# One row-tiled stretch a step for both score blocks, with the down products ahead of it, in a fused attention and GEGLU kernel

## The chip, the core and the metric

The kernel runs on one NeuronCore of a Trainium2 chip. The metric is the device time of one execution in microseconds. Five engines work side by side, each through its own instructions in order: TensorE (PE, with its weight loads shown as PEld), VectorE (DVE), ScalarE (ACT), GpSimd (POOL) and SyncE (SP), which here issues the DMAs. Matrix products land in PSUM, which has eight banks of 512 float32 words per partition. DVE and ACT empty them.

## What is computed

```python
g = sigmoid((x * gate_w).sum(-1, keepdims=True))     # x: 2048 x 576
a = A(x, wq, wk, wv, wo, beta)                       # 32 heads of 18, 4 segments of 512
b = (gelu(x @ w_gate) * (x @ w_up)) @ w_down         # inner width 4608
return g * a + (1 - g) * b

# A, for each segment s
logits = q @ k.T * scale + causal_mask               # 512 x 512 per head
a_dot  = softmax(logits) @ v
a_mem  = (phi(q) @ M) / (phi(q) @ z + 1e-6)          # memory of the segments before
o      = sigmoid(beta) * a_mem + (1 - sigmoid(beta)) * a_dot
M, z   = M + phi(k).T @ v, z + phi(k).sum()
# a = o @ wo
```

Inputs are float32. The kernel splits each float32 operand into a high and a low float16 word and adds three products (high by high, high by low, low by high).

## The kernel before

A first part projects q, k and v and makes the segment memories. Then comes the main part that the change touches: 72 calls of `step(v)`, two for each of the 36 strips of 128 columns of the inner width (`f, p = divmod(v, 2)`). Step v works on strip f and on token chunks c = 2p and e = 2p + 1, of 512 tokens each. Two strips, so four steps, are a block of weights: `fb, i4 = divmod(v, 4)`, with i4 = 0 to 3 the step's place in the block.

The gate and up products use sums and differences of weights and tokens (a Strassen-like scheme), collected in three PSUM banks: X (tag G), Y (tag U) and V. Each `product` call is six matmuls of 512 columns: two blocks of rows k by three word pairs. The last 64 rows of the width 576 come through `rest` (whole array, `x[:, 8]`) and `low_rests`: the low word of the weights takes only 64 of the array's 128 rows, so that two such products, on rows 0 to 63 and 64 to 127, can run beside each other. `gelu` (ACT) and `hidden` (DVE) finish the strip for chunks c and e in tiles g0 and g1 (`gl`, three buffers), and `hidden_pair` splits the result into words hh: the high one on ACT, the low one on POOL.

Into the steps is woven:

- **Down products** of the block before: `down`, six matmuls of 288 columns each into a `dn` bank (two buffers) and one DVE operation that adds the result to `acc`. Eight a step, through `chains`.
- **Attention.** In step v the head and half-sequence with k = v - LAG (LAG is 2) is worked on, with two score blocks a = 2k and b = 2k + 1. `scores` makes four products of 54 rows (three stacked words of 18) with 512, 384, 256 and 128 columns, on rows from 0 or from 64, so two run beside each other. `piece` on DVE adds the mask, takes the row maximum into `mx` and writes to `pf` (two buffers). `powers` is, on ACT, a small operation `mb` on the maxima and four exponentials in place in `pf`. `pair_rows` splits them into words `ph` (ACT the high, POOL the low one), `turn_rows` transposes these by two DMAs into `pt` (two buffers), `values` multiplies them with v into bank `pv` (20 matmuls of 37 columns for a block), and `normalize` (DVE) divides and adds to `ob`. `result_high` and `result_low` split finished rows of `ob`.
- **Weights** for the next strips: `weights_first` (POOL scales them in steps i4 = 0 and 2 and forms the sums in steps 1 and 3, with one scaling of `rawd` in each of steps 2 and 3), `weights_high` (ACT) and `weights_low` (POOL). `act_squares` (ACT) and `scales` (PE, DVE), in step 1 with `scales_out` (POOL), make their scales.

The order on PE, ACT, DVE and POOL is the order of the code (`manual_schedule`), by hand. DMAs on SP are placed by the scheduler. In a step before, low last rows of V and Y (L1095) and the scores of block a stand in one row-tiled stretch in mid-step, and low last rows of X and of Y's last term UG, with the scores of block b, in another at the end. The pieces of a are emptied in the same step, those of b at the start of the next, where the two `hidden` of the step before stand too (`end_pair`).

Of the kernel before, what the change touches and what calls it, by code (L numbers as in the profile page):

```python
# [13 lines left out]
OP = mybir.AluOpType  # L14
# [4 lines left out]
P = 128  # L19
D = 576  # L20
F = 4608
H = 32
DH = 18
L = 512
# [18 lines left out]
def kernel(ctx: ExitStack, tc: tile.TileContext, xs, wqk, wv, wo, wgu, wd, beta, out):  # L43
# [8 lines left out]
    def bank(tag, bufs=1, dt=F32):  # L52
        return ps.tile([P, 512 if dt == F32 else 1024], dt, name=tag, tag=tag, bufs=bufs)
# [77 lines left out]
    x16 = {}  # L131
# [758 lines left out]
    with tc.tile_pool(name="keep", bufs=2, side="right", reuse_waits="tile") as kp, ExitStack() as tail:  # L890
# [25 lines left out]
        def load_v(gg):  # L916
            if gg >= H // 2:
                return
            hf, g = divmod(gg, H // 4)
            vts[gg] = ap_.tile([P, 8, 4 * VC], F16, name="vt", bufs=2)  # L920
            sp.dma_start(vts[gg], vps[hf][:, g * 4 * VC : (g + 1) * 4 * VC].rearrange("(t p) c -> p t c", p=P))
# [11 lines left out]

        COL = [0, P, 3 * P, 6 * P, 10 * P]

        PIECES = ((3, 0), (2, 64), (1, 64), (0, 0))

        def scores(a):

            k, e = divmod(a, 2)  # L940
            q, kt = qts[k], kts[k]
            mx[a] = ap_.tile([P, 4], F32, name="mx", bufs=2)
            prob[a] = ap_.tile([P, 10 * P], F32, name="pf", bufs=2)
            put = []
            for i, (qi, r) in enumerate(PIECES):
                h, n = slice(r, r + 3 * DH), (qi + 1) * P
                o = bank("st" if i < 2 else "dn", 2)[:, :n]
                pe.matmul(o, q[h, e * L + qi * P : e * L + (qi + 1) * P], kt[h, e * L : e * L + n],  # L948
                          start=True, stop=True)
                put.append((qi, o))  # L950

            def piece(i):
                qi, ov = put[i]
                dve.tensor_tensor_reduce(prob[a][:, COL[qi] : COL[qi + 1]], ov, mask[:, L - (qi + 1) * P :],  # L954
                                         1.0, -3e38, OP.add, OP.max, mx[a][:, qi : qi + 1])

            return piece

        def powers(a):

            p = prob[a]
            b = ap_.tile([P, 4], F32, name="mb", bufs=2)
            c = 2 * (a // (2 * H)) + a % 2
            act.activation(b, mx.pop(a), AF.Copy, bias=LN256, scale=esc[:, 1, c : c + 1])  # L964
            for qi in (3, 0, 2, 1):
                r = p[:, COL[qi] : COL[qi + 1]]
                act.activation(r, r, AF.Exp, bias=b[:, qi : qi + 1], scale=esc[:, 0, c : c + 1])  # L967
# [12 lines left out]
        def turn_rows(a):  # L980
            prob.pop(a)
            t, h = turned_p[a], pairs16.pop(a)
            for i in range(2):
                sp.dma_start(t[:, 10 * i : 10 * i + 10], h[:, i], transpose=True)

        def values(a):
            kk, e = divmod(a, 2)
            if e == 0:
                pvb[kk] = bank("pv")
            o = pvb[kk]  # L990
            pr = turned_p.pop(a)
            v = vts[kk // 4]
            c0 = (kk % 4) * VC
            for qi in range(4):
                ov = o[:, (4 * e + qi) * VC : (4 * e + qi + 1) * VC]
                for kb in range(qi + 1):
                    for i in range(2):
                        pe.matmul(ov, pr[:, 10 * i + COL[qi] // P + kb], v[:, 4 * e + kb, c0 : c0 + VC],  # L998
                                  start=kb == 0 and i == 0, stop=kb == qi and i == 1)
# [54 lines left out]
        def chains(b, js):  # L1054
            for j in js:
                down(b, j // 2, j % 2)
                if j % 8 == 7:
                    for ff in (2 * b, 2 * b + 1):
                        hp.pop((ff, j // 8))
                        if j == 31:  # L1060
                            pair_d.pop(ff)
# [14 lines left out]
        def gl_tile():  # L1076
            return mp2.tile([P, L], F32, name="gl", bufs=3)

        def product(o, f, a, x, h, l, start=False, part=range(6)):

            w = pair_g[f]
            for n in part:
                k, (i, b) = n // 3, ((0, h), (0, l), (1, h))[n % 3]
                pe.matmul(o, w[:, i, (a + k) * P : (a + k + 1) * P], x[:, b + k],  # L1084
                          start=start and n == 0, stop=n == 5, skip_group_check=True)
# [11 lines left out]
        def weights_first(fb, i4):  # L1097
            n0 = 2 * fb
            if i4 == 0 and fb:
                scale_g(n0 + 1)  # L1100
            if i4 == 1 and fb:
                sums_g(n0 + 1)
            if i4 == 2 and fb:
                scale_g(n0 + 2)
                scale_d(n0)
            if i4 == 3 and fb:
                sums_g(n0 + 2)
                scale_d(n0 + 1)

        def weights_high(fb, i4):  # L1110
            n0 = 2 * fb
            high_g(n0 + 1 + i4 // 2, i4 % 2)
            if i4 >= 2:
                high_d(n0 + i4 - 2)
# [7 lines left out]
        def weights_load(fb, i4):  # L1122
            n0 = 2 * fb
            if i4 == 1:
                load_g(n0 + 4)
            if i4 == 2:
                load_d(n0 + 2)
            if i4 == 3:
                load_v(fb + 1)
                load_g(n0 + 5)  # L1130
                if not fb:
                    load_d(n0 + 3)
            if i4 == 0 and fb > 1:
                load_d(n0 + 1)

        def act_squares(v):

            fb, i4 = divmod(v, 4)
            todo = {0: ((fb + 1, 2 * fb, 2),),
                    1: ((fb + 1, 2 * fb + 3, 0), (fb + 1, 2 * fb + 3, 1), (fb + 1, 2 * fb + 1, 2)),  # L1140
                    2: ((fb + 2, 2 * fb + 4, 0), (fb + 2, 2 * fb + 4, 1))}
            todo = todo.get(i4, ()) if fb else ()
            if v == 4:
                todo += (2, 4, 0), (2, 4, 1)
            for b, f, i in todo:
                squares(b, f, i, act_square)
# [3 lines left out]
        def first_product(v):  # L1150
            f, p = divmod(v, 2)
            V = bank("V")
            product(V, f, S3, xt[p], 8, 10, True)
            return V
# [3 lines left out]
        def end_pair(between=()):  # L1158

            for i, g in enumerate(ends):  # L1160
                hidden(*g)
                if i == 0:
                    for put in between:
                        put()
            for f, c, o, g in ends:
                hidden_pair(f, c, g)
            ends.clear()

        def step(v):

            f, p = divmod(v, 2)
# [8 lines left out]

            done = (k - 5) // 4 if i4 == 3 and 0 <= (k - 5) // 4 < H // 2 else None
            low = (k - 6) // 4 if i4 == 0 and 0 <= (k - 6) // 4 < H // 2 - 1 else None
            first, middle = {3: ((), ()), 4: ((0,), (1,)), 5: ((2, 3), (4,))}.get(
                v, ((2 * k - 3,) * on(k - 2), (2 * k - 2,) * on(k - 1)))
            x1, x2_, t = x16[c], x16[e], xt[p]
            X, Y = bank("G"), bank("U")
            if v in ahead:
                V, g1 = ahead.pop(v), gl_tile()
                dve.tensor_copy(g1, V)
                end_pair()  # L1190
                act_squares(v)
            else:
                end_pair([lambda i=i: put(2 * k - 1, i) for i in (2, 3)])
                act_squares(v)
                V, g1 = first_product(v), gl_tile()
                dve.tensor_copy(g1, V)
# [12 lines left out]
            for w in {3: (B21, BR), 4: (T3, T4)}.get(v - LAST, ()):  # L1209
                low_w(w)  # L1210
            put(2 * k - 1, 1)
            if v < 4:
                put(2 * k - 1, 2)
                put(2 * k - 1, 3)
            puts.pop(2 * k - 1, None)
# [272 lines left out]
        LAG = 2  # L1488
        LAST = 2 * H + LAG + 1
        with tc.manual_schedule(engines=ORDERED):  # L1490
            for v in range(2 * NF):
                step(v)

                if v == LAST:
                    atn.close()
                    op_ = tail.enter_context(tc.tile_pool(name="outp", bufs=2, side="right", reuse_waits="tile"))
                if v >= LAST:
                    for t in {0: (0, 1), 1: (2, 3), 2: (4, 5), 3: (6,)}.get(v - LAST, ()):
                        turned(t)
                    if v < LAST + 2:  # L1500
                        finish(v - LAST)
            sums_high(1)
            sums_low(1)
            end_pair()


            fb = NB - 1
            for u in range(8):
                unit(u)
                for t in (2 * u + 7, 2 * u + 8):  # L1510
                    if t < 16:
                        turned(t)
                if u < 6:
                    sums_o(u + 2)
                    sums_high(u + 2)
                    sums_low(u + 2)
# [40 lines left out]
```

## Time and profile before

| | |
|---|---|
| Median of 3 runs | 1570.52 us (1570.18 to 1570.59) |
| The profiled execution | 1570.53 us, span 1568.8 us |
| TensorE clock granted | 1.00 |
| Matmuls | 11902 |
| Step start to step start, v = 8 to 65 | 18.22 to 18.36 us |
| A block of four steps | 73.03 us |
| DMA queue of SP, share of 16 engines | 72.3% |

Step starts are read as the first matmul of the product S3 into V in each step. A matmul's busy time in the profile includes its way through the array, so two that follow each other overlap; how often one starts is read from the chain of waits, which shows a run of matmuls with the time until the next one.

### The profile page before, as it was taken

How to read it: one execution, taken by the hardware profiler on the slowest of the kernel's cores; microseconds unless marked ns; L12 is line 12 of the kernel's file. 1: busy time of each engine (PE TensorE's matmuls, PEld its weight loads, DVE VectorE, ACT ScalarE, POOL GpSimd, SP SyncE). 2: the span in 40 equal slices, each digit the busy share in tenths (PEclk: the TensorE clock that was granted, in tenths of full speed). 3: DMA queues.
4: the chain of work that ended last, by engine and by line, in shares of the span. 5: the costliest groups of instructions: out<-in, count | busy, mean ns of one | idle time of the engine just before them, and what ended most of it. 6: DMA issues, size and time to landing. Idle time of an engine off the chain costs nothing.

```text
span 1568.8 us, 32695 instructions
## 1 busy us (share of the span) xinstructions
PE 1563.5 (100%) x11902; PEld 922.2 (59%) x11902; DVE 1142.5 (73%) x2995; ACT 1177.6 (75%) x1973; POOL 1219.1 (78%) x1164
## 2 busy tenths in 40 slices
PE   9999999999999999999999999999999999999999
PEld 6665754555555555555555555555555555555577
DVE  7688876777777777777777767777776777776766
ACT  6667648888879798888888887879888888874310
POOL 3344867888888879797978888887879797887774
PEclk9999999999999999999999999999999999999999
DMA  6633445787979797878788897969797889736162
GB/s 224 221 125 110 140 149 93 126 143 121 147 121 142 118 157 129 142 131 128 130 132 143 126 146 124 147 122 159 112 155 134 136 133 129 139 76 143 32 146 97
DMA packets 472305, 209.00 MB, mean 133 GB/s; under 512 B 427600, under 2 KB 437072, under 8 KB 471632
## 3 DMA queue, kind: packets, MB, share of 16 engines
q1 hardware_dynamic: 472144, 206.92, 72.3%
q8 instruction: 93, 1.52, 0.4%
q14 instruction: 68, 0.56, 0.1%
HBM read 90.99 MB, written 27.26 MB: 75 GB/s over the span
## 4 chain that ended last, share of the span: by engine, by line
PE 98%; ACT 1%; DMA 0%; DVE 0%; issue 0%; SPq 0%; ACTq 0%
PE dn L1044 27%; PE U L1084 18%; PE G L1084 12%; PE V L1084 12%; PE pv L998 4%; PE st L333 3%; PE U L1090 2%; PE G L333 2%; PE dn L342 2%; PE G L1095 1%; PE V L1095 1%; PE U L333 1%; PE st L948 1%; PE U L1437 1%; PE V L1090 1%; PE G L1090 1%
## 5 line engine op out<-in xcount | busy, mean ns | idle before, releaser
L1044 PE MATMUL dn<-paird,hh 128*128 128x288 f16 x3408 | 485.9, 286 | 0.0
L978 POOL TENSOR_TENSOR ph<-pf,ph 128x512 f16<-128x512 f32 (+1 forms) x256 | 353.9, 1404 | 166.6 <-ACT ph L977 166.5
L1084 PEld LDWEIGHTS <-pairg 128*128 128x128 f16 x3024 | 274.8, 98 | 282.3 <-issue 33.0
L1044 PEld LDWEIGHTS <-hh 128*128 128x128 f16 x3456 | 337.7, 98 | 155.8 <-issue 0.2
L1052 DVE SCALAR_TENSOR_TENSOR acc<-dn,ev,acc 128x288 f32<-128x288 f32 x536 | 275.1, 514 | 65.9 <-PE dn L1044 65.4
L967 ACT ACTIVATE pf<-pf,mb,esc 128x512 f32<-128x512 f32 (+3 forms) x512 | 292.9, 642 | 7.0 <-ACT mb L964 0.4
L1084 PE MATMUL G<-x,pairg 128*128 128x512 f16 x864 | 222.0, 380 | 0.5 <-DVE gl L1066 0.4
L1084 PE MATMUL U<-xt,pairg 128*128 128x512 f16 x864 | 210.0, 379 | 0.0
L313 POOL TENSOR_TENSOR pairg<-raw,pairg 128x640 f16<-128x640 f32 (+2 forms) x144 | 175.1, 1238 | 4.0 <-ACT pairg L309 4.0
L1071 POOL TENSOR_TENSOR hh<-gl,hh 128x512 f16<-128x512 f32 x144 | 163.9, 1158 | 16.2 <-ACT hh L1070 16.2
L977 ACT ACTIVATE ph<-pf 128x512 f16<-128x512 f32 (+1 forms) x256 | 172.4, 720 | 0.0
L309 ACT ACTIVATE pairg<-raw 128x640 f16<-128x640 f32 (+2 forms) x144 | 89.9, 651 | 103.3 <-POOL raw L303 54.7
L1250 DVE COPY gl<-U 128x512 f32<-128x512 f32 x72 | 49.8, 692 | 160.8 <-PE U L1084 148.2
L954 DVE CUSTOM_DVE_ANT_0 pf<-st,mask 128x512 f32<-128x512 f32 (+1 forms) x256 | 156.9, 614 | 0.0
L278 POOL TENSOR_SCALAR raw<-raw,sc 128x640 f32<-128x640 f32 x72 | 135.5, 1894 | 0.0
L1084 PE MATMUL U<-x,pairg 128*128 128x512 f16 x432 | 126.9, 378 | 0.0
L1074 ACT ACTIVATE gl<-gl,sc 128x512 f32<-128x512 f32 x144 | 96.6, 715 | 39.4 <-DVE gl L1283 28.2
L954 DVE CUSTOM_DVE_ANT_0 pf<-dn,mask 128x256 f32<-128x256 f32 (+1 forms) x256 | 80.7, 353 | 59.9 <-PE dn L948 59.9
L1070 ACT ACTIVATE hh<-gl 128x512 f16<-128x512 f32 x144 | 85.7, 619 | 28.1 <-DVE gl L1066 27.9
L1084 PE MATMUL V<-xt,pairg 128*128 128x512 f16 x432 | 105.7, 381 | 0.0
L1084 PE MATMUL V<-x,pairg 128*128 128x512 f16 x432 | 104.8, 378 | 0.0
L998 PEld LDWEIGHTS <-pt 128*128 128x128 f16 x2560 | 83.2, 96 | 6.3
(304 smaller groups left out, 2627.4 us busy)
## 6 DMA issues: line engine op xcount, KB each, us to landing
raw<-in_wgu_dram SPq DMA_DIRECT2D x36, 640.0 KB
rawd<-in_wd_dram SPq DMA_DIRECT2D x36, 288.0 KB
qk<-stage SPq DMA_DIRECT2D x36, 256.0 KB
qt<-qk SPq DMA_DIRECT2D x128, 72.0 KB
kt<-qk SPq DMA_DIRECT2D x128, 72.0 KB
vp<-vstage SPq DMA_DIRECT2D x16, 296.0 KB
vt<-vp SPq DMA_DIRECT2D x16, 296.0 KB
qt<-qk SPq DMA_DIRECT2D x128, 36.0 KB
```

Of the source, the lines that this page charges most:

```text
L278: pool.tensor_scalar(r, r, scl[f // 2][0][:, 0:1], None, OP.mult)
L313: pool.tensor_tensor(spot(f, *p, 1), raw_g[f][:, p[0] : p[1]], spot(f, *p, 0), OP.subtract)
L954: dve.tensor_tensor_reduce(prob[a][:, COL[qi] : COL[qi + 1]], ov, mask[:, L - (qi + 1) * P :], 1.0, -3e38, OP.add, OP.max, mx[a][:, qi : q ...
L967: act.activation(r, r, AF.Exp, bias=b[:, qi : qi + 1], scale=esc[:, 0, c : c + 1])
L977: act.activation(h[:, 0, cols], p[:, cols], AF.Copy)
L978: pool.tensor_tensor(h[:, 1, cols], p[:, cols], h[:, 0, cols], OP.subtract)
L998: pe.matmul(ov, pr[:, 10 * i + COL[qi] // P + kb], v[:, 4 * e + kb, c0 : c0 + VC], start=kb == 0 and i == 0, stop=kb == qi and i == 1)
L1044: pe.matmul(o[:, :NH], hh[:, a, q * P : (q + 1) * P], w[:, b, n * NH : (n + 1) * NH], start=i == 0, stop=i == 5)
L1052: dve.scalar_tensor_tensor(av, o[:, :NH], ev, av, OP.mult, OP.add)
L1071: pool.tensor_tensor(hh[:, 1], t, hh[:, 0], OP.subtract)
L1074: act.activation(t, o, AF.Gelu_apprx_tanh, scale=scl[f // 2][0][:, 2 + c : 3 + c])
L1084: pe.matmul(o, w[:, i, (a + k) * P : (a + k + 1) * P], x[:, b + k], start=start and n == 0, stop=n == 5, skip_group_check=True)
```

## The change

A new function `paired_step(v)` takes the place of `step(v)` for v from LAG + 3 = 5 to LAST - 2 = 65 (LAST is 67). In it:

- Low last rows of V and Y, all products of both score blocks, and the low last rows of X stand in one row-tiled stretch. Pieces share banks: the narrow ones lie two to a bank, over both `st` banks, both `dn` banks and `pv`.
- Low last rows of UG are made by `rest` on the whole array.
- All eight down products and the value products of blocks 2k - 4 and 2k - 3 stand ahead of the stretch.
- Both `hidden` and `hidden_pair` of a step are in the step itself. `hidden` of X stands on DVE ahead of three of the four pieces of block a, and its `hidden_pair` ahead of `powers(a)`.
- `scales` comes between the down products, `load_v` behind the values.

```diff
-        def scores(a):
+        def score(a):
...
+            outs = {}
+            def product(i, r, o):
+                h, n = slice(r, r + 3 * DH), (4 - i) * P
+                pe.matmul(o, q[h, e * L + n - P : e * L + n], kt[h, e * L : e * L + n], start=True, stop=True)
+                outs[i] = o
             def piece(i):
...
+            return product, piece
+        def scores(a):
+            product, piece = score(a)
+            for i, r in PIECES:
+                product(i, r, bank("st" if i < 2 else "dn", 2)[:, : (4 - i) * P])
             return piece
...
+        def paired_step(v):
...
+            if ends:
+                end_pair([lambda i=i: put(i) for i in (2, 3)])
+            V, g1 = first_product(v), gl_tile()
+            dve.tensor_copy(g1, V)
+            act_squares(v)
+            product(X, f, A11, x1, 0, 4, True)
+            put(0)
+            dve.tensor_copy(Y, X)
+            put(1)
+            put(3)
+            late(0, 2)
+            values(2 * k - 4)
+            weights_first(fb, i4)
+            powers(2 * k - 1)
+            pair_rows(2 * k - 1, 0)
+            pair_rows(2 * k - 1, 1)
+            turn_rows(2 * k - 1)
+            weights_high(fb, i4)
+            weights_low(fb, i4)
+            weights_load(fb, i4)
+            product(V, f, A22, x2_, 0, 4)
+            rest(V, f, G4, x1, (0,))
+            late(2, 4)
+            if low is not None:
+                result_low(low)
+            product(Y, f, S2, t, 4, 6)
+            g0 = gl_tile()
+            dve.tensor_copy(g0, Y)
+            late(4, 6)
+            if i4 == 1:
+                scales(fb + 1)
+                scales_out(fb + 1)
+            values(2 * k - 3)
+            normalize(k - 2)
+            late(6, 8)
+            if i4 == 3:
+                load_v(fb + 1)
+            product(Y, f, S1, t, 0, 2)
+            rest(Y, f, G4, x2_, (0,))
+            low_rests(f, (V, G4, x1), (Y, G4, x2_))
+            (one, put1), (two, put2) = score(a), score(b)
+            s0, s1, d0, d1, o = bank("st", 2), bank("st", 2), bank("dn", 2), bank("dn", 2), bank("pv")
+            one(0, 0, d1)
+            one(1, 64, o[:, : 3 * P])
+            one(3, 64, o[:, 3 * P :])
+            two(0, 0, s0)
+            one(2, 64, d0[:, : 2 * P])
+            two(2, 64, d0[:, 2 * P :])
+            low_rests(f, (X, U4, x1))
+            two(1, 64, s1[:, : 3 * P])
+            two(3, 64, s1[:, 3 * P :])
+            puts[b] = put2
+            dve.tensor_tensor(g1, Y, g1, OP.add)
+            gelu(f, e, g1, g1)
+            dve.tensor_tensor(g0, V, g0, OP.add)
+            gelu(f, c, g0, g0)
+            put1(2)
+            put2(2)
+            product(X, f, A12, x1, 2, 6)
+            rest(X, f, U4, x1, (0,))
+            hidden(f, c, X, g0)
+            hidden_pair(f, c, g0)
+            put1(0)
+            put1(1)
+            put1(3)
+            product(Y, f, S4, x2_, 2, 6)
+            rest(Y, f, UG, x2_)
+            hidden(f, e, Y, g1)
+            powers(a)
+            pair_rows(a, 0)
+            pair_rows(a, 1)
+            turn_rows(a)
+            if done is not None:
+                result_high(done)
+            hidden_pair(f, e, g1)
+            load_head(k + 2)
...
-                step(v)
+                (paired_step if LAG + 3 <= v < LAST - 1 else step)(v)
```

`put` is the pieces of block 2k - 1 from the step before, and `late(i, j)` is down products i to j of the step. In the steps that stay in `step`, the value products move by one step, so that both blocks of a pair stand together there too.

More of the change, by code (lines that the diff above doesn't have):

```diff
@@ L934 @@
         COL = [0, P, 3 * P, 6 * P, 10 * P]
-        PIECES = ((3, 0), (2, 64), (1, 64), (0, 0))
-        def scores(a):
+        PIECES = ((0, 0), (1, 64), (2, 64), (3, 0))
+        def score(a):
             k, e = divmod(a, 2)
@@ L943, in scores @@
             prob[a] = ap_.tile([P, 10 * P], F32, name="pf", bufs=2)
[L944 to L950, printed above, removed]
-            def piece(i):
-                qi, ov = put[i]
-                dve.tensor_tensor_reduce(prob[a][:, COL[qi] : COL[qi + 1]], ov, mask[:, L - (qi + 1) * P :],
-                                         1.0, -3e38, OP.add, OP.max, mx[a][:, qi : qi + 1])
+            outs = {}
[3 more added lines that the diff above has]
+                outs[i] = o
+            def piece(i):
+                if i in outs:
+                    qi = 3 - i
+                    dve.tensor_tensor_reduce(prob[a][:, COL[qi] : COL[qi + 1]], outs.pop(i), mask[:, L - (qi + 1) * P :],
+                                             1.0, -3e38, OP.add, OP.max, mx[a][:, qi : qi + 1])
+            return product, piece
[3 more added lines that the diff above has]
+                product(i, r, bank("st" if i < 2 else "dn", 2)[:, : (4 - i) * P])
             return piece
@@ L1128, in weights_load @@
             if i4 == 3:
-                load_v(fb + 1)
+                if not fb or n0 + 2 > LAST // 2:
+                    load_v(fb + 1)
                 load_g(n0 + 5)
@@ L1167, in end_pair @@
             ends.clear()
+        def paired_step(v):
+            f, p = divmod(v, 2)
+            fb, i4 = divmod(v, 4)
+            c, e = 2 * p, 2 * p + 1
+            k = v - LAG
+            a, b = 2 * k, 2 * k + 1
+            late = lambda i, j: chains(fb - 1, range(8 * i4 + i, 8 * i4 + j))
+            put = puts.pop(2 * k - 1)
+            done = (k - 5) // 4 if i4 == 3 and 0 <= (k - 5) // 4 < H // 2 else None
+            low = (k - 6) // 4 if i4 == 0 and 0 <= (k - 6) // 4 < H // 2 - 1 else None
+            x1, x2_, t = x16[c], x16[e], xt[p]
+            X, Y = bank("G"), bank("U")
+            if ends:
[34 more added lines that the diff above has]
+            if i4 == 3:
+                load_v(fb + 1)
+            product(Y, f, S1, t, 0, 2)
[37 more added lines that the diff above has]
+            load_head(k + 2)
+            if i4 == 2:
+                load_ob(fb)
@@ L1182, in step @@
             low = (k - 6) // 4 if i4 == 0 and 0 <= (k - 6) // 4 < H // 2 - 1 else None
-            first, middle = {3: ((), ()), 4: ((0,), (1,)), 5: ((2, 3), (4,))}.get(
-                v, ((2 * k - 3,) * on(k - 2), (2 * k - 2,) * on(k - 1)))
+            first, middle = {4: ((0,), (1,))}.get(v, ((2 * k - 4, 2 * k - 3) if v > 4 and on(k - 2) else (), ()))
             x1, x2_, t = x16[c], x16[e], xt[p]
@@ L1192, in step @@
             else:
-                end_pair([lambda i=i: put(2 * k - 1, i) for i in (2, 3)])
+                if ends:
+                    end_pair([lambda i=i: put(2 * k - 1, i) for i in (2, 3)])
                 act_squares(v)
@@ L1211, in step @@
             put(2 * k - 1, 1)
-            if v < 4:
+            if v < 4 or v == LAST - 1:
                 put(2 * k - 1, 2)
```

## The prediction

> **What bounds the kernel now.** I read the page first, then a table by stage, then the chain of waits, then ACT's and POOL's rows in order of time.
>
> ```profile
> PE 1563.5 (100%) x11902; PEld 922.2 (59%) x11902; DVE 1142.5 (73%) x2995; ACT 1177.6 (75%) x1973; POOL 1219.1 (78%) x1164
> PE 98%; ACT 1%; DMA 0%; DVE 0%; issue 0%; SPq 0%; ACTq 0%
> 696.64:714.86 18.22, 18.22 (x150) 10.47 (x147) 13.85 (x38) 16.69 (x29) 14.71 (x11) 1.00 0.94 182
> 714.86:733.21 18.35, 18.35 (x151) 10.70 (x148) 13.73 (x43) 16.30 (x30) 13.48 (x13) 1.00 0.87 143
> 733.21:751.44 18.23, 18.23 (x149) 10.46 (x147) 13.11 (x37) 14.40 (x25) 17.22 (x18) 1.00 0.73 96
> 751.44:769.67 18.23, 18.23 (x150) 10.48 (x147) 13.11 (x37) 14.44 (x24) 16.45 (x17) 1.00 0.67 112
> 696.64:769.67 73.03, 73.03 (x590) 42.11 (x587) 53.80 (x152) 61.83 (x104) 61.85 (x58) 1.00 0.80 134
> ```
>
> The four middle rows are one block, steps with i4 = 0, 1, 2, 3. Columns: length, then busy time of PE, PEld, DVE, ACT, POOL. PE is busy throughout and the chain that ended last is PE's: today the time is the length of PE's own stream. But ACT and POOL work 61.8 us of 73.03, and in step 2 POOL works 17.22 of 18.23. A change that shortens PE's stream has little room before another engine's order decides.
>
> **The PE stream.** The chain of waits, start, length, group; first a whole-array run, then the two stretches of one step:
>
> ```profile
> 705.57 1.29 PE U L1084 x6
> 706.86 0.21 PE U L1090
> 707.08 0.32 PE V L1095
> 707.40 0.16 PE st L948
> 707.56 0.11 PE dn L948
> 707.67 0.76 PE G L1084 x3
> ...
> 714.33 0.32 PE G L1095
> ...
> 714.92 1.41 PE V L1084 x6
> ```
>
> Six whole products of 512 columns take 1.29, so 0.215 each. A stretch lasts from its low last rows to the next whole product, 0.59 (707.08 to 707.67, 714.33 to 714.92), and makes the products behind it late: three take 0.76 instead of 0.65, six take 1.41 instead of 1.29. It costs 0.70 and 0.71, 1.41 a step. Its columns, 512+512+128 on one half of the rows beside 512+384+256 on the other, are 1152, or 0.48 at the rate above; 0.22 is the price of leaving and re-entering whole-array work.
>
> After the change one stretch carries 4 x 512 columns on one half (low rows of V, two widest score pieces, low rows of X) and 512 + 384+128 + 256+256 + 384+128 on the other: 2048 each, 0.86, plus 0.22 once: 1.08. The low last row of UG loses its partner and becomes a whole product, 0.215. That makes 1.30 against 1.41, **-0.11 a step**. `paired_step` runs for v = 5 to 65, 61 steps: -6.7 us. The trace has no stretch with pieces of 128 and 256 columns in this order; if their weight loads are hidden entirely and the switch is halved, it is -0.22 a step, if each half pays a second switch, +0.11. I take -0.11, since the old stretch mixed 512, 384, 256 and 128 too. The down products, value products and everything else on PE are the same in number; they only move.
>
> The Trainium skill (TensorE: Matmul & The Clock Gate, Back-to-back issue gap) gives about 131 ns per 512-column product in a sustained stream. The rows say 215; by the page's figure the extra product would cost 0.13 and the step would gain 0.20 instead of 0.11.
>
> **The loop through ACT, POOL and DVE.** PE does not stand in it, so it shows as no wait of PE yet. ACT, then POOL, in order of time:
>
> ```profile
> 709.55 1.34 ACT L1074 ACTIVATE gl<-gl,sc 128x512 f32<-128x512 f32 x2
> 727.22 1.33 ACT L1074 ACTIVATE gl<-gl,sc 128x512 f32<-128x512 f32 x2 [0.51 <-DVE gl L1283]
> 729.33 0.30 ACT L964 ACTIVATE mb<-mx,esc 128x4 f32<-128x4 f32 x1 [0.77 <-DVE mx L954]
> 748.04 1.33 ACT L1074 ACTIVATE gl<-gl,sc 128x512 f32<-128x512 f32 x2
> 749.28 0.28 ACT L964 ACTIVATE mb<-mx,esc 128x4 f32<-128x4 f32 x1
> 749.58 1.28 ACT L967 ACT_TABLE_LOAD   x1
> 750.88 2.29 ACT L967 ACTIVATE pf<-pf,mb,esc 128x512 f32<-128x512 f32 x4
> 753.07 1.35 ACT L977 ACTIVATE ph<-pf 128x512 f16<-128x512 f32 x2
> 766.28 1.33 ACT L1074 ACTIVATE gl<-gl,sc 128x512 f32<-128x512 f32 x2
> ```
> ```profile
> 733.82 2.76 POOL L978 TENSOR_TENSOR ph<-pf,ph 128x512 f16<-128x512 f32 x2 [4.50 <-ACT ph L977]
> 736.55 0.23 POOL L250 TENSOR_SCALAR sc<-v 128x2 f32<-128x2 f32 x1
> ...
> 738.32 2.28 POOL L1071 TENSOR_TENSOR hh<-gl,hh 128x512 f16<-128x512 f32 x2
> ...
> 753.76 2.76 POOL L978 TENSOR_TENSOR ph<-pf,ph 128x512 f16<-128x512 f32 x2 [1.55 <-ACT ph L977]
> ...
> 756.77 2.27 POOL L1071 TENSOR_TENSOR hh<-gl,hh 128x512 f16<-128x512 f32 x2
> ...
> 766.95 2.52 POOL L313 TENSOR_TENSOR pairg<-raw,pairg 128x640 f16<-128x640 f32 x2
> ```
>
> Follow step 2 into step 3: both gelus (748.04), mb, table load, four exponentials, ACT's copy of the pair (753.07), POOL's two subtractions (753.76), POOL's two for hh (756.77), POOL's scaling or sums of the weights (`weights_first`), ACT's high words of these weights, its table load, and the next gelus (766.28). ACT and POOL are in order, so each waits for the one before. From gelu to gelu:
> - into step 3: 766.28 - 748.04 = 18.24, against a PE step of 18.23. This loop is already full.
> - into step 0: 709.55 + 73.03 - 766.28 = 16.30.
> - into step 1: 727.22 - 709.55 = 17.67, of which 0.51 was a wait for DVE: 17.16.
> - into step 2: 748.04 - 727.22 = 20.82, less 0.77 waiting for mx and less POOL's scalars of `scales_out`, 738.32 - 736.55 = 1.77, which the change puts ahead of hh and off this path: 18.28.
>
> Together 69.98 for a block in which PE needs 73.03.
>
> What the change does to it. Before, mb of block a followed the gelus at once (748.04 to 749.28, 1.24), as DVE had taken the scores beside them. Now `put1(0)`, `put1(1)` and `put1(3)` stand on DVE behind `hidden(f, c, X, g0)`, and that waits for the second gelu. DVE in order of time:
>
> ```profile
> 697.54 0.28 DVE L954 CUSTOM_DVE_ANT_0 pf<-dn,mask 128x128 f32<-128x128 f32 x1
> ...
> 697.75 0.74 DVE L1066 SCALAR_TENSOR_TENSOR gl<-U,sc,gl 128x512 f32<-128x512 f32 x1
> 698.42 0.68 DVE L1196 COPY gl<-V 128x512 f32<-128x512 f32 x1
> ...
> 709.48 0.68 DVE L954 CUSTOM_DVE_ANT_0 pf<-st,mask 128x512 f32<-128x512 f32 x1
> 710.09 0.08 DVE L954 DVE_READ_ACCUMULATOR2_ANT mx<- 128x1 f32 x1
> ...
> 710.52 0.55 DVE L954 CUSTOM_DVE_ANT_0 pf<-st,mask 128x384 f32<-128x384 f32 x1
> 710.99 0.08 DVE L954 DVE_READ_ACCUMULATOR2_ANT mx<- 128x1 f32 x1
> ```
>
> So behind the gelus, 1.33, come hidden 0.67 (697.75 to 698.42), the pieces of 512 (0.61), 384 (0.47) and 128 columns (0.28), and two handovers between engines that I estimate at 0.07 each from gaps between these rows: 3.50 until mb, where it was 1.24: +2.26. In return one of POOL's two hh subtractions runs while ACT makes the exponentials and leaves the path: -1.13 (half of 2.27). Net **+1.13 a step**: 17.4, 18.3, 19.4, 19.4, a block of 69.98 + 4.52 = **74.50**.
>
> PE's block would be 73.03 - 0.44 = 72.59. The loop is longer, and nothing lets it run ahead: `put2(2)` needs pf's buffer (two in all), which POOL frees only after the same `weights_first` and its subtraction of block 2k-1; on DVE hidden X and all else wait behind it. So the block takes 74.50, 1.47 more than now, and 61 steps are 15.25 blocks: +22.4 us. Against the profiled execution (1570.53 with a span of 1568.8; the median shown, 1570.52, is the same) that is **1593**. PE's own gain is inside, not added: PE waits.
>
> Where it waits: ACT's and POOL's lag grows over steps 2 and 3 by 1.3 each (19.4 against 18.1). POOL's hh subtraction of g1 now ends behind both pair subtractions and holds one of three gl buffers, for which the copy of Y to g0 on DVE waits; behind that stand the evictions of the next down products, and PE finds both dn banks full. And POOL wrote the low words of the next strip by 769.47 (766.95 + 2.52), 0.2 before the step that starts at 769.67; with the lag the third product of S3 waits. Steps 0 and 1 give the lag back.
>
> **Edits that cost nothing.** All eight down products in front: four more evictions fall into DVE's first half, where it sat idle; in step 1 the product of `scales` takes a dn bank between them, at most one eviction's time of waiting, which the loop covers. Values of 2k-4 beside 2k-3 leave three transposed blocks for two pt buffers, so the transposes wait on SP for values. Today a block is in use soon after POOL finishes it:
>
> ```profile
> 746.68 0.51 PE pv L998 x20
> ```
>
> That is 10.1 after 736.58 (733.82 + 2.76). In the new order block 2k is finished about 8 to 10 into the next step and used 4.7 into the one after: some 13 us, enough, and its buffer is free by then. Head loads behind it on SP have more than a step. If this cover were gone, PE would pay the difference in each step. `load_v` moves to where its buffer comes free; it is needed a block later.
>
> **Rivals.**
> 1. *Loop longer than PE* (forecast, 1585 to 1602): per-step addition of 0.9 to 1.3, with the gaps between engines as the unknown. Against: ACT and POOL each idle 11 us per block.
> 2. *PE's stream decides, faster*: if the addition is under (72.59 - 69.98) / 4 = 0.65, because work of ACT or POOL overlaps more than I see, the loop hides and only -0.11 is left: 1570.5 - 6.7 = 1564, between 1557 and 1567. That needs half of the three put pieces and hidden off the path; the code's DVE order speaks against it.
> 3. *Lag costs twice*: PE pays 74.50 - 72.59 = 1.9 of a lag of 2.6 in steps 2 and 3. If the S3 wait does not lie beside the wait for dn banks but behind it, it pays the other 0.7 too: 75.2, +33, 1604, and more where other buffers join.
> 4. *In between*: an addition of 0.65 to 0.9 gives 72.6 to 73.6 a block: 1564 to 1580, the only way to a tie.
>
> **How the numbers follow.** About 0.2% (3.1 us) can be told from no change. Forecast 0.55; PE's stream 0.23; lag twice 0.12; in between 0.10, which I split into 0.06 same, 0.03 slower and 0.01 faster. Slower: 0.55 + 0.12 + 0.03 = 0.70; faster 0.24; same 0.06. The range has to reach the faster case, of which it takes most, and most of the heavy one: 1563 to 1606, leaving out some 0.17. The likeliest case alone is 1585 to 1602.
>
> **What would show it.** Right: one stretch a step of about 1.08 plus the 0.215 product; PE waits of 1 to 2 us a block at dn products behind DVE and at S3 behind POOL's pairg, none in step 2; POOL's wait for ACT ph in every step; gelu to gelu 19.4 in steps 2 and 3. Wrong: a block of 72.6 with PE unbroken (rival 2), a stretch of over 1.3, or PE waiting for pt from DMA.

## The result, and the profile after

| | before | after |
|---|---|---|
| Median, us | 1570.55 (4 runs) | 1590.76 (4 runs) |
| Ratio, 95% interval | | 1.0128 (1.0111 to 1.0146) |
| Span of the profiled execution, us | 1568.8 | 1589.1 |
| A block of four steps, us | 73.03 | 74.52 or 74.23 |

The change costs 20.2 us; 22.4 were forecast. From the page of the changed kernel, busy time and the chain that ended last:

```profile
PE 1563.7 (98%) x11902; PEld 937.8 (59%) x11902; DVE 1158.2 (73%) x2995; ACT 1179.7 (74%) x1973; POOL 1225.9 (77%) x1164
PE 37%; POOL 26%; ACT 23%; DVE 7%; issue 5%; DMA 2%; SPq 1%; POOLq 0%; ACTq 0%; DVEq 0%
```

PE, ACT and POOL work at most 7 us longer than before and DVE 16, and the number of matmuls is the same. But the chain, which was 98% PE, now runs through POOL, ACT and DVE for more than half of the span. The table by stage, for the steps i4 = 0, 1, 2, 3 of one block and the block (length, then busy time of PE, PEld, DVE, ACT, POOL):

```profile
1075.22:1094.74 19.52, 18.29 (x147) 10.68 (x146) 15.27 (x40) 16.22 (x27) 17.10 (x13) 1.00 0.87 149
1094.74:1113.20 18.46, 18.46 (x150) 10.91 (x149) 14.30 (x44) 16.43 (x29) 14.49 (x15) 1.00 0.93 145
1113.20:1131.31 18.11, 18.11 (x147) 10.76 (x146) 12.25 (x35) 15.66 (x27) 15.25 (x17) 1.00 0.70 125
1131.31:1149.45 18.14, 18.14 (x147) 10.79 (x146) 12.84 (x34) 13.63 (x23) 15.24 (x15) 1.00 0.67 114
1075.22:1149.45 74.23, 73.00 (x587) 43.15 (x586) 54.66 (x151) 61.95 (x104) 62.07 (x57) 1.00 0.80 133
```

Steps 2 and 3 are 0.09 to 0.12 shorter than before, so PE's gain is there. Step 0 has a hole. PE in order of time, at the start of step 0, and who PE waited for in the whole run:

```profile
1075.22 0.59 PE L1091 MATMUL V<-xt,pairg 128*128 128x512 f16 x2
1077.05 1.04 PE L1091 MATMUL V<-xt,pairg 128*128 128x512 f16 x4 [1.23 <-POOL pairg L313]
```
```profile
PE V L1091 <- POOL pairg L313: 20.1, 15, 1.5
```

Two products of S3 go, the third needs the low word of the next strip, and that POOL finishes late: one wait a block, 15 in all. Two products take 0.43, so the third could have started at 1075.65; it starts at 1077.05, and 1.40 are lost. Read alone, this says that POOL is slow with `weights_low`. The chain of waits says why. From the scaling of weights in step 2 to the gelus of step 3 (start, length, group; short pieces left out):

```profile
1126.36 1.71 POOL rawd L317
...
1128.09 0.68 ACT paird L321
...
1128.80 1.28 ACT L1081
...
1130.09 1.34 ACT gl L1081 x2
...
1131.46 0.75 DVE gl L1073
1132.21 0.60 DVE pf L954
...
1133.54 0.30 ACT mb L971
...
1133.86 1.28 ACT L974
...
1137.44 0.53 ACT ph L984
...
1138.04 2.75 POOL ph L985 x2
1140.79 1.12 POOL hh L1078
...
1145.42 1.71 POOL rawd L317
...
1149.15 1.34 ACT gl L1081 x2
```

This is the loop of the forecast, with no PE in it: gelus, hidden X on DVE (L1073), the pieces of the scores (L954), mb, table load, exponentials, POOL's pair, one hh, weights, and the next gelus. From gelu to gelu it takes 1149.15 - 1130.09 = 19.06.

A second reading needs no experiment. In the first half of the steps `load_ob` also makes POOL clear part of `ob` once a block (L930), in the second half it does not. Windows of one block of each half, the changed kernel, then before, and the clearing itself:

```profile
628.85:703.37 74.52, 73.00 (x587) 43.10 (x586) 54.71 (x151) 61.97 (x105) 62.40 (x58) 1.00 0.77 131
```
```profile
600.00:673.03 73.03, 73.03 (x589) 42.09 (x587) 53.81 (x153) 61.84 (x104) 61.87 (x58) 1.00 0.81 134
1117.00:1190.03 73.03, 73.03 (x587) 42.10 (x586) 53.68 (x152) 61.73 (x104) 61.57 (x57) 1.00 0.91 136
```
```profile
L930 POOL MEMSET ob<- 128x288 f32 x1 | 0.3, 329 | 0.0
```

0.33 us of POOL work cost nothing before; after the change it makes the block 0.29 longer, 74.52 against 74.23. What stands in the binding loop is paid nearly in full.

### The profile page after: what moved, and what is told of

It reads as the page before. It is cut to its first block, busy times and chain, and to the rows that moved or that the text cites. A ratio compares the mean times of both kernels' runs of the same rounds, so it can differ in the third digit from the quotient of the medians.

```text
span 1589.1 us, 32678 instructions
## 1 busy us (share of the span) xinstructions
PE 1563.7 (98%) x11902; PEld 937.8 (59%) x11902; DVE 1158.2 (73%) x2995; ACT 1179.7 (74%) x1973; POOL 1225.9 (77%) x1164
## 4 chain that ended last, share of the span: by engine, by line
PE 37%; POOL 26%; ACT 23%; DVE 7%; issue 5%; DMA 2%; SPq 1%; POOLq 0%; ACTq 0%; DVEq 0%
POOL ph L985 8%; PE dn L1051 7%; ACT pf L974 6%; POOL raw L278 6%; PE U L1091 4%; ACT gl L1081 4%; ACT L974 4%; ACT L1081 4%; DVE pf L954 4%; PE G L1091 3%; PE V L1091 3%; POOL rawd L317 3%; POOL hh L1078 3%; PE st L333 3%; DVE gl L1073 2%
## 5 line engine op out<-in xcount | busy, mean ns | idle before, releaser
L1091 PEld LDWEIGHTS <-pairg 128*128 128x128 f16 x3024 | 283.1, 98 | 335.5 <-POOL pairg L313 27.5
L1051 PE MATMUL dn<-paird,hh 128*128 128x288 f16 x3408 | 465.9, 286 | 0.0
L1051 PEld LDWEIGHTS <-hh 128*128 128x128 f16 x3456 | 333.0, 98 | 124.6 <-DVE pb L244 0.3
L1059 DVE SCALAR_TENSOR_TENSOR acc<-dn,ev,acc 128x288 f32<-128x288 f32 x536 | 264.5, 514 | 120.1 <-PE dn L1051 119.7
L1091 PE MATMUL G<-x,pairg 128*128 128x512 f16 x864 | 212.0, 380 | 0.5 <-DVE gl L1073 0.4
L1078 POOL TENSOR_TENSOR hh<-gl,hh 128x512 f16<-128x512 f32 x144 | 174.4, 1213 | 14.7 <-ACT hh L1077 14.7
L954 DVE CUSTOM_DVE_ANT_0 pf<-dn,mask 128x256 f32<-128x256 f32 (+1 forms) x195 | 95.8, 497 | 87.7 <-POOL ph L985 83.6
L1091 PE MATMUL U<-x,pairg 128*128 128x512 f16 x432 | 107.3, 379 | 0.0
L954 DVE CUSTOM_DVE_ANT_0 pf<-st,mask 128x512 f32<-128x512 f32 (+2 forms) x195 | 95.1, 512 | 0.0
L1005 PE MATMUL pv<-vt,pt 128*128 128x37 f16 x2560 | 84.3, 179 | 0.0
```

Source lines behind the costliest of these rows:

```text
L1051: pe.matmul(o[:, :NH], hh[:, a, q * P : (q + 1) * P], w[:, b, n * NH : (n + 1) * NH], start=i == 0, stop=i == 5)
L1059: dve.scalar_tensor_tensor(av, o[:, :NH], ev, av, OP.mult, OP.add)
L1078: pool.tensor_tensor(hh[:, 1], t, hh[:, 0], OP.subtract)
```

## The experiments

Two theories. **The loop**: the time from gelu to gelu through DVE, ACT and POOL is longer than PE's step. **POOL's queue**: POOL has too much ahead of the low words, and time is lost at S3 alone. Both see the same wait of PE. All edits are of the changed kernel, but for the last two, which are of the first experiment.

### Pieces ahead of hidden X, both hh last

```diff
             put1(2)
-            put2(2)
+            put1(0)
+            put1(1)
+            put1(3)
             product(X, f, A12, x1, 2, 6)
             rest(X, f, U4, x1, (0,))
             hidden(f, c, X, g0)
-            hidden_pair(f, c, g0)
-            put1(0)
-            put1(1)
-            put1(3)
+            put2(2)
...
                 result_high(done)
+            hidden_pair(f, c, g0)
             hidden_pair(f, e, g1)
```

> Edit of the changed kernel: on DVE put1(0), put1(1), put1(3) go ahead of hidden X and put2(2) behind it; hidden_pair of g0 goes behind powers(a). PE's stream is not touched. Theory of the loop (gelu, hidden X, three pieces, mb, exponentials, POOL's pairs and weights, next gelu): hidden X and the three pieces leave the path, +1.13 a step becomes about 0, the loop falls to some 70 a block and PE decides: 18.1 in steps 2 and 3 and 0, 18.4 in step 1 (its scales product), a block of 72.8, 1567 us, no wait at S3. Rival, that POOL simply has too much in its queue in front of the low words of the next strip: POOL does the same work, so 1590 stays.

Measured: 1576.21 us, ratio 1.0033 (1.0020 to 1.0045). POOL does the same work, yet the wait at S3 is gone from the list of PE's waits: the rival falls, and steps 0, 2 and 3 take 18.1 as the loop theory said. But 9 us more than expected are left, all in step 1, which lasts 18.5 to 19.9 (mostly 18.9). The place is `scales`. DVE there, then POOL at that time, then the same operations before the change:

```profile
1094.09 0.52 DVE L241 TENSOR_SCALAR v<-z 128x2 int32<-128x2 int32 x1
1094.52 0.15 DVE L242 TENSOR_SCALAR pb<-dn 128x4 int32<-128x4 int32 x1
1094.64 0.38 DVE L243 TENSOR_SCALAR v<-v 128x2 int32<-128x2 int32 x1
```
```profile
1093.86 0.73 POOL L302 TENSOR_TENSOR raw<-raw 128x256 f32<-128x256 f32 x1
1094.54 0.46 POOL L303 TENSOR_TENSOR raw<-raw 128x128 f32<-128x128 f32 x1
```
```profile
732.49 0.16 DVE L241 TENSOR_SCALAR v<-z 128x2 int32<-128x2 int32 x1
```

An operation on two words a partition takes 0.52 instead of 0.16. It ends at 1094.61, when POOL's L302 has ended (1094.59); L243 ends at 1095.02, when L303 has (1095.00). L242, which reads PSUM, is not held. DVE's next evictions stand behind it, and PE waits for a dn bank:

```profile
PE dn L1051 <- DVE pb L244: 3.2, 12, 0.3
```

The Trainium skill (SBUF — State Buffer, Who interferes with whom) says that VectorE and GpSimd share a pair of ports, and that a VectorE `tensor_scalar` in a two-port mode and a GpSimd instruction shut each other out for a whole instruction. These rows fit, for a POOL operation that holds one of DVE; in which mode L241 runs, they do not show.

### Pieces ahead of hidden X, the buffer's piece still first

```diff
             put1(2)
             put2(2)
+            put1(0)
+            put1(1)
+            put1(3)
...
             hidden_pair(f, c, g0)
-            put1(0)
-            put1(1)
-            put1(3)
```

> Edit of the changed kernel: put1(0), put1(1), put1(3) go ahead of hidden X, but put2(2) stays ahead of them; hidden_pair of g0 stays ahead of powers(a). Theory of the loop, with its second branch: put2(2) waits for the pf buffer that POOL frees last, and the three pieces stand behind it on DVE, so the path from POOL's pair of block 2k-1 over put2(2) to the pieces stays as long: block 74.2 to 74.6, 1587 to 1593. If only the branch over the gelus and hidden X mattered: about 73.0 a block, 1570. Rival of the POOL queue: 1590 as well.

Measured: 1601.38 us, 1.0195 (1.0181 to 1.0209). No gain, as the second branch of the loop demands; but 8 us more than its upper end. The chain of waits of this kernel shows what I had left out:

```profile
1099.81 1.61 POOL ph L985
...
1101.88 0.60 DVE pf L954
1102.49 0.47 DVE pf L954
1102.96 0.20 DVE pf L954
1103.18 0.67 DVE gl L1073
1103.87 0.63 ACT hh L1077
1104.50 0.19 ACT mb L971
```

`put2(2)` waits for POOL's pair of block 2k - 1 (it gives back pf), the pieces follow, and then hidden X and ACT's copy for hh (0.67 and 0.63) still stand ahead of mb, because `hidden_pair` is ahead of `powers(a)` on ACT. So this experiment breaks the branch over hidden X only in part.

### Only the buffer's piece behind

```diff
             put1(2)
-            put2(2)
...
             put1(3)
+            put2(2)
```

> Edit of the changed kernel: on DVE put2(2) goes behind put1(3), so hidden X and the three pieces no longer wait for the pf buffer that POOL frees last; hidden X stays ahead of the pieces and hidden_pair where it was. It breaks the branch over the buffer alone, as the second experiment broke the branch over hidden X alone. If both branches are about equally long: the one over gelu and hidden X keeps the block at 74.0 to 74.4, 1587 to 1592. If the buffer were what binds: 73.0 to 73.3 a block, 1570 to 1575.

Measured: 1590.73 us, 1.0127 (1.0111 to 1.0144): the changed kernel's own time. With the two experiments above: moving the three pieces alone gains nothing, moving the buffer's piece alone gains nothing, and only both moves together make the time fall. The next experiment is the cleaner partner of the second, as it differs from it in the place of `put2(2)` alone.

### Both branches broken, ACT's copy left in place

The first experiment without moving `hidden_pair`.

> Edit of the changed kernel: as the first experiment, but hidden_pair of g0 stays ahead of powers(a), so ACT's copy for it stands between hidden X and mb, while POOL's subtraction stays off the path. Theory of the loop: hidden 0.67 and the copy 0.6 stay on the path and the three pieces leave it (1.36) with POOL's subtraction (1.13): addition over the loop of before about 0.2 a step, under the 0.65 at which PE decides; blocks of 72.8 to 73.2 apart from step 1's hold, 1573 to 1579, close to the first experiment. If hidden X ahead of mb were what binds: 1590.

Measured: 1582.56 us, 1.0072 (1.0059 to 1.0086), 3.6 above the upper end expected, and 18.8 less than the second experiment. Apart from step 1 the block is as expected: step 0 takes 18.3 to 18.6, steps 2 and 3 take 18.1. Most of the rest is step 1, which lasts 19.0 and where L241 takes 0.6. The copy left ahead of mb costs 6.3 us beside the first experiment. The wait at S3 is gone from the list here too, though in the first half 0.24 of it is left (the six products of S3 in 1.70 instead of 1.46).

### Hh of g0 behind the exponentials

The changed kernel with only `hidden_pair(f, c, g0)` moved behind `result_high`.

> Edit of the changed kernel: only hidden_pair of g0 goes behind powers(a), so POOL's subtraction for it stands again behind both pair subtractions, as before the change; DVE's order stays. Theory of the loop: the 1.13 that had left the path is back in every step, the block grows by 4 x 1.1 to 78.5 or 79, 1650 to 1660 us. Rival of the POOL queue: the same work in another order ahead of the same low words, 1590 within some 5.

Measured: 1659.03 us, 1.0562 (1.0546 to 1.0578). 68 us more than the changed kernel, or 1.12 in each of 61 steps: what one POOL subtraction of hh takes in the chain above (1.12). Each of the four loops grows by it: gelu to gelu into steps 0 to 3 of a block takes 19.05, 19.07, 20.40 and 20.20, against 17.92, 17.96, 19.27 and 19.06 in the changed kernel. An order of POOL's work that looks harmless is worth its full length once per step. The same move was worth 6.3 us the other way round in the first experiment, where hidden X and the pieces had left the path.

### Low words first

`pair_rows` gets an argument for making the high or the low words alone; the other steps keep their order.

```diff
...
+            if i4 == 3:
+                pair_rows(2 * k - 1, 0, "high")
+                pair_rows(2 * k - 1, 1, "high")
+                weights_high(fb, i4)
+                weights_low(fb, i4)
+                pair_rows(2 * k - 1, 0, "low")
+                pair_rows(2 * k - 1, 1, "low")
+                turn_rows(2 * k - 1)
...
```

> Edit of the changed kernel: in step 3 POOL makes the low words of weights (L313, L325) ahead of its subtractions for block 2k-1 instead of behind them. The words that PE waits for at S3 are ready 2.7 earlier. Rival of the POOL queue (the time is lost at S3 alone): the wait of 1.4 a block goes, block 72.9 to 73.1, 1569 to 1572. Theory of the loop: the wait at S3 goes, but put2(2) now waits 3.7 longer in step 3 for its pf buffer and hidden X behind it; PE waits for X instead: block 76 to 77.5, 1617 to 1638.

Measured: 1654.94 us, 1.0533 (1.0519 to 1.0548), beyond the upper end of what the loop theory gave. Who PE waits for, PE in order of time around one such wait, and the step:

```profile
PE G L1093 <- DVE gl L1075: 53.8, 16, 4.0
```
```profile
1115.87 1.46 PE L1093 MATMUL V<-xt,pairg 128*128 128x512 f16 x6
1120.72 2.50 PE L1093 MATMUL G<-x,pairg 128*128 128x512 f16 x6 [3.39 <-DVE gl L1075]
```
```profile
1115.87:1139.36 23.49, 20.10 (x147) 11.36 (x146) 16.35 (x43) 16.39 (x27) 17.69 (x13) 0.93 0.81 143
```

And who DVE waits for in this kernel (total, times, longest):

```profile
DVE pf L954 <- POOL ph L987: 114.7, 45, 6.5
```

The wait at S3 is gone, and a longer one for X stands in its place: hidden X is behind `put2(2)` on DVE, and that waits for POOL's pair (L954 for L987, up to 6.5 us). Taking away the visible wait of PE cost 64 us. The rest of the miss fits the clock: after 3.4 us without work the granted clock of this step is 0.93, the six products take 2.50 instead of 1.46, and PE is busy 20.10 in the step instead of 18.1. That is 2.0 a block, where the time is 17 us, or 1.1 a block, beyond the upper end.

### Scales at the end of the step, or in another bank

To the first experiment, two ways to meet what was left in step 1.

```diff
-            if i4 == 1:
-                scales(fb + 1)
-                scales_out(fb + 1)
             values(2 * k - 3)
...
             hidden(f, e, Y, g1)
+            if i4 == 1:
+                scales(fb + 1)
+                scales_out(fb + 1)
             powers(a)
```

> Edit of the first experiment (pieces ahead of hidden X): scales and scales_out move from between the down products to the end of step 1. Theory that the rest of its loss (step 1 lasts 18.5 to 19.9 instead of 18.1) comes from two DVE operations of scales (L241, L243, both operands in SBUF) that end only when POOL's sum in flight ends, with the dn bank held meanwhile: at the step's end POOL waits for ACT and not one of them is held, they take 0.16 each, step 1 lasts 18.1 to 18.3, a block 72.6, 1564 us. Rival, that step 1 is held by ACT's squares or the product of scales itself: 1576 stays.

The other way; `scales` takes the bank as an argument:

```diff
...
-                scales(fb + 1)
+                scales(fb + 1, bank("st", 2))
```

> Edit of the first experiment: scales stays between the down products, but its product goes to an st bank instead of a dn bank. If PE is held by the shared dn bank alone, step 1 falls to 18.2 and the time to 1564 or 1565, with L241 and L243 still at 0.4 to 0.7. If the late DVE itself holds PE (the evictions of the next down products stand behind scales), step 1 stays at 18.4 or more and the time between 1567 and 1574.

Measured at the end of the step: **1566.42 us, 0.9972 (0.9961 to 0.9983)**, faster than the kernel before. Its rival falls. It is 2.4 above the 1564 expected; in a few blocks step 0 or step 1 is 0.2 to 0.7 longer than in the rows below. In another bank: 1571.05, 0.9999 (0.9989 to 1.0008); DVE is still held and step 1 mostly lasts 18.5 to 18.6, so the bank was half of it and the late DVE the other half. The kernel with `scales` at the end, by stage, and its L241 in order of time:

```profile
1131.48:1149.59 18.11, 18.11 (x147) 10.76 (x146) 14.27 (x38) 15.12 (x26) 16.40 (x12) 1.00 0.81 154
1149.59:1167.85 18.26, 18.26 (x149) 10.99 (x148) 13.50 (x38) 16.37 (x29) 13.49 (x13) 1.00 0.98 134
1167.85:1185.96 18.11, 18.11 (x149) 10.76 (x148) 13.74 (x41) 15.84 (x28) 15.99 (x17) 1.00 1.00 164
1185.96:1204.10 18.14, 18.14 (x147) 10.79 (x146) 13.46 (x37) 14.47 (x24) 16.28 (x16) 1.00 0.64 95
1131.48:1204.10 72.62, 72.62 (x587) 43.30 (x586) 54.97 (x152) 61.81 (x104) 62.16 (x57) 1.00 0.86 137
```
```profile
1096.29 0.16 DVE L241 TENSOR_SCALAR v<-z 128x2 int32<-128x2 int32 x1
```

PE is busy in the whole block again, at 72.62 against 73.03, and DVE's small operation is back at 0.16.

## Why the prediction was right, point by point

- **PE's stream, -0.11 a step.** Right. One stretch in the kernel above, from its chain of waits:

```profile
1145.44 0.32 PE V L1102
...
1146.41 1.40 PE G L1091 x6
```

  0.97 from the low last rows to the next product and 0.11 on the six behind it (1.40 instead of 1.29): 1.08, as worked out. An unbroken block is 72.62; 72.59 was the estimate.
- **The loop, +1.13 a step, 74.50 a block.** Right, and shown by the experiments on its parts. From the gelus to mb it is 3.45 (1133.54 - 1130.09) where 3.50 was worked out. The block is 74.52 with POOL's clearing of `ob`, which was in the loops I measured, and 74.23 without it, which I had not noticed. The clearing lay in the loop into step 3 of the kernel before:

```profile
756.47 0.33 POOL L930 MEMSET ob<- 128x288 f32 x1
```

  Without it, 19.1 is the forecast for the 19.06 measured into step 3. That the sum came out to 0.02 is partly luck. The gelus of the four steps start at 1092.86, 1110.82, 1130.09 and 1149.15, behind 1074.94. So the loops are 17.92, 17.96, 19.27 and 19.06, where 17.4, 18.3, 19.4 and 19.1 were worked out: the first is 0.5 too long, the second 0.3 too short. In step 0 a DVE operation of `result_low`, which stands elsewhere now, meets POOL's hh:

```profile
1084.80 1.45 DVE L1034 SCALAR_TENSOR_TENSOR oh<-ob,wsc,oh 128x576 f16<-128x576 f32 x1
1085.60 1.68 POOL L1078 TENSOR_TENSOR hh<-gl,hh 128x512 f16<-128x512 f32 x1
```

  The hh takes 1.68 instead of 1.16 and ends 1.02 behind the DVE operation; both hold within 0.02 in all 15 blocks, but no run moves that operation to prove it the cause. Into step 1 the sum took 1.24 from gelu to mb in the kernel before, where it was 1.55 (711.10 - 709.55): mb had waited for DVE there, and the forecast left that wait in. The block is longer than before by 1.49 in the first half and 1.20 in the second; the mean over 15.25 blocks is 20.5 us, and 20.2 were measured.
- **The bounds of the likeliest case.** An addition of 0.9 a step gives 1579 by the same sum, not 1585, which belongs to 1.0. The measured 1590.76 lies inside both readings.
- **Two branches that both keep the loop closed** (over hidden X, and over pf and `put2(2)`). Right: the time stayed or rose when one was mended, and fell by 18.8 when `put2(2)` moved in the kernel whose three pieces stood ahead of hidden X.
- **Where PE waits.** Half wrong. I named two places, the dn banks behind a late copy to g0 and S3. Only S3 waits. The step that failed is that POOL's hh of g1 holds the gl buffer which the copy to g0 needs. In the trace that copy (L1217) waits for PE's Y in 44 of its 46 waits, and it runs before hh of g1 is done:

```profile
1140.43 0.69 DVE L1217 COPY gl<-U 128x512 f32<-128x512 f32 x1 [0.84 <-PE U L1091]
1140.76 1.16 POOL L1078 TENSOR_TENSOR hh<-gl,hh 128x512 f16<-128x512 f32 x1
```

  So it takes another buffer, that of g0 of the step before, whose hh was done by 1135.37 (1134.22 + 1.15). The run with hh of g0 behind the exponentials agrees: there the copy starts 0.03 us after the first of the two subtractions, that of g0, ends. In that run the wait of the forecast does appear: the copy waits for POOL's hh 59 times (100.4 us), and PE waits for a dn bank behind DVE 29 times (28.4 us). In the changed kernel the sum did not depend on it, since the loop sets the block's length wherever PE feels it.
- **Edits at no cost.** The product of `scales` between the down products costs 0.20 in step 1 (18.46 against 18.26 with it at the end), inside the bound of one eviction, and covered by the loop. Its cover gone, in the first experiment, the same place cost mostly 0.65 (18.91 instead of 18.26) and up to 1.6 (19.86), through the hold by POOL that I had not foreseen. PE does not wait for pt in the changed kernel.

## What to carry to other kernels

An engine that is busy all the time bounds the kernel only as long as every loop through the others is shorter than its step. Measure such a loop in the trace, from one instruction to the same one a step later, with the waits for others taken out, and add to it what a new order puts between; here the loop had no room in two of four steps before anything was changed. And the place where the busy engine ends up waiting need not be the place to mend: moving POOL's low words forward took that wait away and cost 64 us, while a new order of five operations on the loop removed it and gained 14.6.

## What the runs showed of the hardware that was not expected

- DVE operations of two words a partition between SBUF tiles took up to 0.7 us instead of 0.16 in the first experiment, when POOL was at work on SBUF, and the held ones ended within 0.03 of POOL's operation; one that reads PSUM was not held (0.15).
- A DVE operation between SBUF tiles of 1.45 us and a POOL subtraction begun during it: the subtraction took 1.68 instead of 1.16, in every block of the changed kernel.
- One wait of 3.4 us slowed PE for the products behind it (six in 2.50 instead of 1.46, mean clock of the step 0.93), while waits of 1.4 in the changed kernel left the clock at 1.00.
